# Attention and channel mix on one core: twelve pairs' scores from uncut float32, key-weight work moved to GpSimd, key products from step 7, sums in tiles of their own

## The chip, the cores and the metric

The kernel runs on one NeuronCore of a Trainium2 chip. The metric is the device time of one execution in microseconds (us), the median of three runs: 1001.76 us for the kernel before.

## The reference

```python
def _attn_ref(q, k, v, cap):                       # (8, 12, 448, 64) each
    scale = 1.0 / np.sqrt(q.shape[-1])
    scores = scale * np.matmul(q, k.transpose(0, 1, 3, 2))
    scores = cap * np.tanh(scores / cap)
    scores = scores - np.max(scores, axis=-1, keepdims=True)
    attn = np.exp(scores)
    attn = attn / (np.sum(attn, axis=-1, keepdims=True) + 1e-09)
    return np.matmul(attn, v)
def _moe_ref(x, mu_k, mu_r, w_k, w_v, w_r):        # x: (8, 448, 768)
    x_prev = np.concatenate([np.zeros((B, 1, D)), x[:, :-1, :]], axis=1)
    xk = mu_k * x + (1.0 - mu_k) * x_prev
    xr = mu_r * x + (1.0 - mu_r) * x_prev
    k = np.maximum(xk @ w_k, 0.0)                  # w_k: 768 x 1024
    v = k * k @ w_v                                # w_v: 1024 x 768
    r = 1.0 / (1.0 + np.exp(-(xr @ w_r)))          # w_r: 768 x 768
    return r * v
```

The attention's result, heads side by side, is the x of the second part. The three weight matrices arrive as float64 and are rounded to float32 on the chip.

## The kernel before

**Steps.** Two heads make a pair; 8 batches of 6 pairs give 48 pairs. `run` goes through 54 steps. Step i computes the scores of pair i, the product with the values of pair i-1, and the normalisation and mixing of pair i-2. What a step issues, and in what order, is written out in the strings `EVEN` and `ODD`; every engine works through its own share in that order.

**Scores.** Keys lie on the partitions of the result: three groups `g` of 128 keys (`scores`, L200) and a left group of 64 keys, done for two pairs at once in even steps (`scores_left`, L212). Each half of 64 partitions is one head. The operands are cut in a high and a low part of reduced precision (F32R) by `qk_high` and `qk_low` on GpSimd (for the first pair on VectorE), two steps ahead, and a group is three products: high x high, low x high, high x low. The left group and the product with the values (`values`, L237) use full float32, which the profile shows as two instructions per product. Scores stand in two PSUM tiles that take turns.

**Softmax.** ScalarE does tanh (L218) and exp (L228) of each group over 896 columns; VectorE sums blocks of 32 columns in transposed form (`red`, L252). `gather` (four DMAs on SP's queue at the head of the next step) brings the four partition blocks of the sums together, `recip` adds and inverts them, `rec_store` and `rec_load` spread the result through DRAM, and `norm` (L281) scales the values product. Sums of two pairs share one tile `r1`, and two such tiles take turns.

**Mixing and keys.** `mix_old` (ScalarE, L291) and `mix_new` (VectorE) make xk of the pair; `x_high` and `x_low` cut it on GpSimd (tiles `xkh`, `xkl`). The key products (`kpart`, L331) run over 8 column blocks `fc` of w_k, 6 pairs `dc` and 3 parts: 144 for each batch, 1152 in all. The order inside a batch takes, for the first two blocks, the products of the first five pairs first (15 + 15), then those of the sixth. Four groups of key products, written `K`, stand in each step, and `key_split` says how many products each holds. Two PSUM tiles take turns for the sums over `dc`; ScalarE empties each with a relu.

**Weights.** The weights come in 44 pieces of 128 x 384, 16 of them of w_k. Every step loads one (`weight_load`), `more` loads a second one in some odd steps. ScalarE takes the absolute value at the step's end, VectorE rounds in five operations in the next step (`weight_round`, one for each `f`, the rest in `weight_rest`; L390 is the clamp), GpSimd adds the low word and copies the high part of w_k (`weight_sum`, L405), and VectorE makes its low part one step later (`weight_low`, L418). One tile `wt` holds the clamped value.

**Second phase.** After the steps 28 chunks of 128 rows compute r and v (L474) and the output. `Body(maxima=True)` is a second path for larger caps; it does not run with these inputs.

Of the kernel before, what the change touches and what calls it, by code (L numbers as in the profile page):

```python
# [25 lines left out]
P = 128  # L26
# [11 lines left out]
QM = S + KM  # L38
QA = QM + KL
NSTEP = NPAIR + 6  # L40
HALF = (slice(0, 64), slice(64, 128))
NB = 2 * S // 32

# [8 lines left out]
ODD = """gather load_v weight_load more weight_low S0 S1 V S2 f f f f f weight_rest tanh0 exp0 red0  # L52
# [8 lines left out]
class Body:  # L61
# [61 lines left out]
    def init_sums(self, pool):  # L123


        nc = self.nc
        self.r1, self.sq, self.sr = [], [], []
        for j in range(2):
            self.r1.append(pool.tile([P, 7, NB], F32, name=f"r1_{j}"))
            sq = pool.tile([32, 4, 4, NB], F32, name=f"sq_{j}")  # L130
            g, q = (0, 0) if j else (3, 2)
            nc.gpsimd.memset(sq[:, q + 1, g], 0.0)
            nc.vector.tensor_copy(sq[:, q, g], self.grd[0:32].to_broadcast([32, NB]))
            self.sq.append(sq)
            self.sr.append(pool.tile([32, 32], F32, name=f"sr_{j}"))
            nc.gpsimd.memset(self.sr[j], 1.0)

    def init_attn(self):
        self.raw, self.QK, self.rawv, self.S, self.P32, self.PV, self.R, self.rs = ({} for _ in range(8))
# [30 lines left out]

    def row_maxima(self, i):

        nc, qk, raw = self.nc, self.QK[i], self.raw[i]
        m = self.up.tile([S // 4, 8], F32, name="m", bufs=1)
        for h in range(2):
            t = HALF[h]
            for c in range(4):
                if c % 2 == 0:
                    s = self.ps_s.tile([P, 2, 512], F32, name="s")
                o = s[0:S // 4, c % 2, 0:S]  # L180
                q = slice(c * S // 4, (c + 1) * S // 4)
                for n, (a, b) in enumerate(((0, 0), (1, 0), (0, 1))):
                    nc.tensor.matmul(o[:, 0:KM], qk[b][t, q], qk[a][t, S:QM], start=(n == 0), stop=(n == 2))
                nc.tensor.matmul(o[:, KM:S], raw[t, q], raw[t, QM:QA], start=True, stop=True)
                nc.vector.reduce_max(m[:, 4 * h + c:4 * h + c + 1], o, axis=mybir.AxisListType.X)
        nc.scalar.activation(m, m, AF.Tanh, scale=self.scl_t[0:S // 4])
        nc.vector.tensor_scalar(m, m, self.cap_t[0:S // 4], None, op0=ALU.mult)
        nc.sync.dma_start(self.max_d.rearrange("h (c p) -> p (h c)", c=4), m)
        M = self.M[i] = self.rawp.tile([P, 2, S], F32, name="M")
        for h in range(2):  # L190
            nc.sync.dma_start(M[:, h], self.max_d[h:h + 1, :].to_broadcast([P, S]))

    def scores(self, i, g):
        nc, qk = self.nc, self.QK[i]
        s = self.ps_s.tile([P, 2, 512], F32, name="s")
        k = slice(S + g * P, S + (g + 1) * P)

        for n, (a, b) in enumerate(((0, 0), (1, 0), (0, 1))):
            for h, p in enumerate(HALF):
                nc.tensor.matmul(s[:, h, 0:S], qk[a][p, k], qk[b][p, 0:S], start=(n == 0), stop=(n == 2))  # L200
        if g == 2:
            self.QK.pop(i)
        self.S[i, g] = s

    def scores_left(self, i):


        s = self.ps_s.tile([P, 2, 512], F32, name="s")
        for p in range(2):
            raw = self.raw.pop(i + p)  # L210
# [38 lines left out]


    def red(self, i, g):
        self.nc.vector.tensor_reduce(out=self.r1[i // 2 % 2][:, 3 if g == "L" else i % 2 * 4 + g],  # L252
                                     in_=self.P32[i, g].rearrange("p h (b k) -> p (h b) k", k=32),
                                     axis=mybir.AxisListType.X, op=ALU.add, apply_transpose=True)

    def gather(self, i):
        r1, sq = self.r1[i // 2 % 2], self.sq[i % 2]
        for q in range(4):
            left = int(q // 2 == i % 2)
            g, w = (4 - left, 3 + left) if i % 2 else (0, 3 + left)  # L260
            self.nc.sync.dma_start(sq[:, q, 4 - w:4] if i % 2 else sq[:, q, 0:w], r1[32 * q:32 * q + 32, g:g + w])  # L261

    def recip(self, i):
        nc, t = self.nc, self.sr[i % 2]
        nc.vector.tensor_reduce(out=t[:, 0:NB], in_=self.sq[i % 2].rearrange("l q g x -> l x q g"),  # L265
                                axis=mybir.AxisListType.XY, op=ALU.add)
# [111 lines left out]
    def weight_round(self):  # L378

        nc = self.nc  # L380
        while True:
            if not self.w_abs:
                yield
                continue
            n, w, sq = self.w_abs.pop(0)
            low, top = w[:, :, 0], w[:, :, 1]
            t = self.wp.tile([P, WC], F32, name="wt")
            a = self.wp.tile([P, WC], U32, name="wa", bufs=3)
            u = t.bitcast(U32)
# [12 lines left out]

    def weight_sum(self, e="p"):
        for n, a, sq in self.w_sum:
            {"p": self.nc.gpsimd, "v": self.nc.vector}[e].tensor_add(sq, f(a), sq)  # L405
            if n < NWK:
                fc, d = divmod(n, ND // 3)
                hi, lo = (x[:, 3 * d:3 * d + 3, fc * P:(fc + 1) * P] for x in (self.WKH, self.WKL))
                sq = sq.rearrange("p (c n) -> p c n", c=3)
                self.copy(e, hi, sq)  # L410
                self.w_low.append((lo, sq, hi))
            else:
                self.w_done.append((n, sq))
        self.w_sum = []

    def weight_low(self):
        for lo, sq, hi in self.w_low:
            self.nc.vector.tensor_sub(lo, sq, f(hi))  # L418
        self.w_low = []

    def weight_store(self):
        for n, sq in self.w_done:
# [71 lines left out]
    def step(self, i):  # L494
# [10 lines left out]
        for op in (EVEN if even else ODD).split():  # L505
# [43 lines left out]
    def run(self):  # L549
# [6 lines left out]
        self.w_raw, self.w_abs, self.w_sum, self.w_low, self.w_done = [], [], [], [], []  # L556
        with ExitStack() as outer:
            def pool(name, bufs, stack=outer, **kw):
                return stack.enter_context(tc.tile_pool(name=name, bufs=bufs, **kw))
# [36 lines left out]
            w2p_a = None  # L596
# [1 line left out]
            for i in range(NSTEP):  # L598
                if i == NPAIR + 1:
                    self.weight_store()  # L600
                    assert self.w_next == NW and not (self.w_raw or self.w_abs or self.w_sum or self.w_low)
                    wst.close()
                    est.close()
                    ast.close()
# [90 lines left out]
```

## Time and profile before

| What | Value |
|---|---|
| Median of three runs | 1001.76 us (1000.11 to 1002.43) |
| Profiled execution, its own time | 1000.05 us |
| Span of the profile, first to last instruction | 998.0 us |
| TensorE busy | 944.5 us (95%) |
| VectorE busy | 650.6 us (65%) |
| ScalarE busy | 488.0 us (49%) |
| GpSimd busy | 278.6 us (28%) |

Busy time is the share in which an engine runs at least one instruction. PE is TensorE's matmuls, PEld its weight loads, DVE VectorE, ACT ScalarE, POOL GpSimd, SP the DMA queue of SyncE. Times in the rows below count from the span's start.

### The profile page before, as it was taken

The page shows a single profiled execution, that of the slowest core. Times are in us where ns is not written, and L with a number is a line of the kernel's source. Part 1 is how long each engine was busy: PE and PEld are TensorE (multiplying, and loading weights), DVE is VectorE, ACT ScalarE, POOL GpSimd, SP SyncE. Part 2 cuts the span into 40 slices and gives each one's busy share as a digit, 9 for nine tenths or more (in the row PEclk, how much of TensorE's full clock was granted, in tenths as well). Part 3 has the DMA queues.
Part 4 walks back from the last instruction along what each step waited for, and adds up shares of the span by engine and source line. Part 5 has one row for each costly group of instructions (what it writes and reads, how often), then busy time and mean ns, then how long its engine had stood idle before and what let it go on. Part 6 is the DMA issues. An engine that isn't in the chain of part 4 may idle for free.

```text
span 998.0 us, 14541 instructions
## 1 busy us (share of the span) xinstructions
PE 944.5 (95%) x5328; PEld 754.1 (76%) x5328; DVE 650.6 (65%) x1128; ACT 488.0 (49%) x578; POOL 278.6 (28%) x267
## 2 busy tenths in 40 slices
PE   7667999999999999999999899999999999999997
PEld 3234655666666656656667799999999999999997
DVE  6998987887877777866555486644654554554460
ACT  6776777887878778867675122212211211221220
POOL 4555564445554545444431320000000000000000
PEclk9788999999999999999999999999999999999999
DMA  4545556665665666654433853323332332332220
GB/s 151 164 146 161 166 156 189 191 202 179 195 200 168 196 194 196 200 180 133 145 125 97 269 166 107 106 75 85 106 92 68 106 107 64 96 106 78 82 69 35
DMA packets 124705, 138.52 MB, mean 139 GB/s; under 512 B 19664, under 2 KB 109776, under 8 KB 124624
## 3 DMA queue, kind: packets, MB, share of 16 engines
q1 hardware_dynamic: 115408, 122.82, 42.3%
q10 hardware_dynamic: 9216, 14.68, 4.0%
q8 instruction: 44, 0.72, 0.3%
q14 instruction: 37, 0.30, 0.1%
HBM read 92.64 MB, written 42.40 MB: 135 GB/s over the span
## 4 chain that ended last, share of the span: by engine, by line
PE 71%; DVE 9%; ACT 7%; DMA 6%; issue 2%; SPq 2%; POOL 2%; ACTq 0%; DVEq 0%; POOLq 0%
PE pvv L474 24%; PE pr L474 18%; PE kps L331 15%; PE s L200 6%; PE pv L237 6%; ACT p L228 3%; ACT p L218 3%; DVE r L252 2%; SPq L261 2%; DMA sq<-r 1%; PE pv L246 1%; DMA r<-rec_d 1%; DVE sr L265 1%; PE s L212 1%; DVE x L281 1%
## 5 line engine op out<-in xcount | busy, mean ns | idle before, releaser
L252 DVE TRANSPOSE_TENSOR_REDUCE r<-p 128x28 f32<-128x896 f32 x144 | 158.2, 1105 | 60.6 <-ACT p L228 60.0
L79 ACT CAST xh<-t 128x768 fp32r<-128x768 f32 x27 | 22.6, 838 | 308.4 <-DVE t L457 308.4
L331 PE MATMUL kps<-xkh,wkh 128*128 128x448 f32 x384 | 142.6, 371 | 18.5 <-POOL xkh L75 15.9
L218 ACT ACTIVATE p<-s,scl_t 128x896 f32<-128x896 f32 x144 | 143.4, 996 | 20.6 <-PE s L200 14.1
L228 ACT ACTIVATE p<-p,cap_t 128x896 f32<-128x896 f32 x144 | 149.9, 1041 | 4.0
L331 PE MATMUL kps<-xkl,wkh 128*128 128x448 f32 x384 | 143.9, 375 | 4.9 <-POOL xkl L85 4.9
L489 DVE TENSOR_TENSOR o<-pvv,rsg 128x768 f32<-128x768 f32 (+1 forms) x29 | 27.0, 930 | 184.3 <-PE pvv L474 183.4
L331 PE MATMUL kps<-xkh,wkl 128*128 128x448 f32 x384 | 143.3, 373 | 0.0
L237 PE MATMUL pv<-p,rv 128*64 128x448 f32 x576 | 128.7, 585 | 4.0 <-DVE xk L296 4.0
L474 PE MATMUL pvv<-wvh,kl 128*128 128x384 f32 x448 | 115.8, 336 | 0.0
L474 PE MATMUL pvv<-wvh,kh 128*128 128x384 f32 x448 | 115.7, 336 | 0.0
L474 PE MATMUL pvv<-wvl,kh 128*128 128x384 f32 x448 | 115.6, 336 | 0.0
L331 PEld LDWEIGHTS kps<-xkh,wkh 128*128 128x128 f32 x384 | 72.6, 189 | 29.4 <-POOL xkh L75 20.4
L85 POOL TENSOR_TENSOR qkl<-rqk,qkh 128x832 fp32r<-128x832 f32 x47 | 92.9, 1976 | 3.9
L237 PEld LDWEIGHTS pv<-p,rv 128*64 128x64 f32 x576 | 39.7, 146 | 71.7 <-issue 58.3
L331 PEld LDWEIGHTS kps<-xkl,wkh 128*128 128x128 f32 x384 | 72.5, 189 | 19.7 <-POOL xkl L85 8.3
L405 POOL TENSOR_TENSOR wsq<-wa,wsq 128x384 f32<-128x384 f32 x44 | 44.4, 1009 | 153.4 <-DVE wsq L398 130.3
L474 PE MATMUL pr<-wrl,xh 128*128 128x384 f32 x336 | 85.9, 336 | 0.0
L474 PE MATMUL pr<-wrh,xl 128*128 128x384 f32 x336 | 85.8, 336 | 0.0
L474 PE MATMUL pr<-wrh,xh 128*128 128x384 f32 x336 | 85.8, 336 | 0.0
L200 PE MATMUL s<-qkh 64*128 64x448 f32 x288 | 66.3, 456 | 19.2 <-ACT p L218 12.4
L200 PEld LDWEIGHTS s<-qkh 64*128 64x128 f32 x288 | 28.5, 193 | 71.5 <-issue 25.0
(73 smaller groups left out, 1565.9 us busy)
## 6 DMA issues: line engine op xcount, KB each, us to landing
rqk<-qk SPq DMA_DIRECT2D x47, 448.0 KB
k_d<-ko ACTq DMA_DIRECT2D x64, 224.0 KB
kr<-k_d SPq DMA_DIRECT2D x28, 512.0 KB
x_d<-x SPq DMA_DIRECT2D x48, 224.5 KB
r<-rec_d SPq DMA_DIRECT2D x96, 112.0 KB
out<-o SPq DMA_DIRECT2D x27, 384.0 KB
xc<-x_d SPq DMA_DIRECT2D x24, 387.0 KB
rv<-v SPq DMA_DIRECT2D x48, 192.0 KB
```

Source lines behind the costliest of these rows:

```text
L79: self.nc.scalar.copy(out, x)
L85: {"p": self.nc.gpsimd, "v": self.nc.vector}[e].tensor_sub(*a)
L200: nc.tensor.matmul(s[:, h, 0:S], qk[a][p, k], qk[b][p, 0:S], start=(n == 0), stop=(n == 2))
L218: self.nc.scalar.activation(p32, self.S.pop((i, g))[:, :, 0:S], AF.Tanh, scale=self.scl_t)
L228: self.nc.scalar.activation(p32, p32, AF.Exp, scale=1.0 if self.maxima else self.cap_t)
L237: nc.tensor.matmul(pv[p, 0:S], v[:, g, h, :], ph[:, h, :], start=(g == 0), stop=False)
L252: self.nc.vector.tensor_reduce(out=self.r1[i // 2 % 2][:, 3 if g == "L" else i % 2 * 4 + g], in_=self.P32[i, g].rearrange("p h (b k) -> p ...
L261: self.nc.sync.dma_start(sq[:, q, 4 - w:4] if i % 2 else sq[:, q, 0:w], r1[32 * q:32 * q + 32, g:g + w])
L331: nc.tensor.matmul(self.kps[fc][:, 0:S], w, m[:, dc, :], start=first, stop=last)
L405: {"p": self.nc.gpsimd, "v": self.nc.vector}[e].tensor_add(sq, f(a), sq)
L474: self.nc.tensor.matmul(ps[:, m, 0:HN], a[:, c, :], w[:, c, m * HN:m * HN + HN], start=(c == 0 and part == 0), stop=(c == n - 1 and part = ...
L489: nc.vector.tensor_mul(o[:, q], pv[:, q, 0:HN], rs[:, q])
```

## The change

Five things change. The scores of pairs 0 to 11 read the uncut float32 tiles (`factors`), one product per group and half in place of three, and their `qk_high` and `qk_low` are not issued. For the 16 pieces of w_k the clamp goes to GpSimd, and the low part is made by GpSimd in `weight_sum`, right after the high part; `weight_low` goes. The second piece of a step is loaded in steps 7, 8, 9 and 10 in place of 1, 3, 5, 7 and 9. The key products begin in the first group of step 7 in place of the third group of step 6, and the groups from step 48 on hold 8 in place of 7. The sums of even and odd pairs get a tile each, with the group index innermost; the left sums of the odd pair are copied across by GpSimd, and the four gathers have one form.

```diff
+UNCUT = 12
-EVEN = """gather load_v load_vl weight_load more weight_low S0 S1 V VL L S2 f f f f f weight_rest tanh0 exp0 red0
+EVEN = """gather load_v load_vl weight_load more S0 S1 V VL L S2 f f f f f weight_rest tanh0 exp0 red0
 (ODD: weight_low taken out in the same way)
@@ init_sums
-            self.r1.append(pool.tile([P, 7, NB], F32, name=f"r1_{j}"))
+            self.r1.append(pool.tile([P, NB, 4], F32, name=f"r1_{j}"))
+            self.sq.append(pool.tile([32, 4, NB, 4], F32, name=f"sq_{j}"))
+        self.lz = pool.tile([P, NB], F32, name="lz")
...
@@ scores, row_maxima
+    def factors(self, i):
+        if i < UNCUT:
+            return (self.raw[i],), ((0, 0),)
+        return self.QK[i], ((0, 0), (1, 0), (0, 1))
-        for n, (a, b) in enumerate(((0, 0), (1, 0), (0, 1))):
+        for n, (a, b) in enumerate(terms):
             for h, p in enumerate(HALF):
-                nc.tensor.matmul(s[:, h, 0:S], qk[a][p, k], qk[b][p, 0:S], start=(n == 0), stop=(n == 2))
+                nc.tensor.matmul(s[:, h, 0:S], qk[a][p, k], qk[b][p, 0:S], start=(n == 0), stop=(n == len(terms) - 1))
@@ red, gather
+        r1 = self.r1[0 if g == "L" else i % 2]
+        self.nc.vector.tensor_reduce(out=r1[:, :, 3 if g == "L" else g],
...
+        if g == "L":
+            self.pcopy(self.r1[1][HALF[1], :, 3], r1[HALF[1], :, 3])
+            self.pcopy(r1[HALF[1], :, 3], self.lz[HALF[1]])
         for q in range(4):
+            self.nc.sync.dma_start(self.sq[i % 2][:, q], self.r1[i % 2][32 * q:32 * q + 32])
@@ weight_round, weight_sum
-            nc.vector.tensor_scalar(t, sq, W_TINY, W_HUGE, op0=ALU.max, op1=ALU.min)
+            e = nc.gpsimd if n < NWK else nc.vector
+            e.tensor_scalar(t, sq, W_TINY, W_HUGE, op0=ALU.max, op1=ALU.min)
...
-                self.w_low.append((lo, sq, hi))
+                self.sub(e, lo, sq, f(hi))
-    def weight_low(self):
-        for lo, sq, hi in self.w_low:
-            self.nc.vector.tensor_sub(lo, sq, f(hi))
@@ step
-                if 0 <= j < NPAIR:
+                if 0 <= j < NPAIR and not (op[:2] == "qk" and j < UNCUT):
-                if i in (1, 3, 5, 7, 9):
+                if i in (7, 8, 9, 10):
                     self.weight_load()
@@ key_split
-        for c in range(26, NSTEP * 4):
+        for c in range(28, NSTEP * 4):
             i = c // 4
-            w = min(7 if i % 2 == 0 or i >= NPAIR else 5, total - n)
+            w = min(8 if i >= NPAIR else 5 if i % 2 else 7, total - n)
@@ run
-            self.qk_high(0, "v")
-            self.qk_low(0, "v")
-            self.qk_high(1)
-            self.qk_low(1)
```

## Rows read from the trace of the kernel before

**Rows 1.** Busy time by stretch; columns: stretch, length, each engine, clock, DMA share, GB/s.

```profile
12.07:82.04 69.97, 46.20 (x242) 20.40 (x243) 63.89 (x104) 51.57 (x60) 39.37 (x41) 0.81 0.48 141
82.04:141.21 59.17, 55.62 (x299) 35.58 (x298) 52.26 (x85) 42.16 (x53) 31.49 (x33) 0.93 0.55 168
141.21:530.71 389.50, 378.44 (x2185) 246.96 (x2184) 290.61 (x441) 301.85 (x358) 187.00 (x169) 0.99 0.58 177
178.33:244.27 65.94, 63.97 (x373) 41.78 (x373) 51.84 (x82) 51.85 (x62) 33.39 (x30) 1.00 0.62 188
...
530.71:556.93 26.22, 22.59 (x118) 15.29 (x117) 10.03 (x16) 9.02 (x12) 5.15 (x7) 1.00 0.45 143
556.93:998.00 441.07, 435.50 (x2464) 432.91 (x2464) 228.66 (x470) 76.75 (x91) 9.91 (x9) 0.99 0.35 99
```

**Rows 2.** TensorE's largest wait over the whole span: total us, times, longest.

```profile
PE kps L331 <- POOL xkh L75: 15.9, 9, 5.6
```

**Rows 3.** ScalarE's waits in the first 155 us.

```profile
ACT pv L291 <- DVE x L281: 22.3, 10, 4.6
...
ACT wsq L370 <- DMA w<-wk: 3.6, 5, 1.5
```

**Rows 4.** Timeline of TensorE, steps 15 to 17: start, us, operation.

```profile
178.33 0.47 PE L200 MATMUL s<-qkh 64*128 64x448 f32 x2
...
179.05 0.37 PE L200 MATMUL s<-qkh 64*128 64x448 f32 x2
...
179.76 2.48 PE L237 MATMUL pv<-p,rv 128*64 128x448 f32 x12
182.16 0.47 PE L200 MATMUL s<-qkh 64*128 64x448 f32 x2
...
187.22 0.47 PE L200 MATMUL s<-qkh 64*128 64x448 f32 x2
...
191.84 0.93 PE L212 MATMUL s<-rqk 64*64 64x448 f32 x8
...
199.38 0.47 PE L200 MATMUL s<-qkh 64*128 64x448 f32 x2
```

**Rows 5.** Timeline of VectorE and ScalarE, step 0 and steps 2 to 4.

```profile
4.74 1.03 DVE L85 TENSOR_TENSOR qkl<-rqk,qkh 128x832 fp32r<-128x832 f32 x1
...
6.98 1.01 ACT L218 ACTIVATE p<-s,scl_t 128x896 f32<-128x896 f32 x1
...
34.84 1.04 ACT L228 ACTIVATE p<-p,cap_t 128x896 f32<-128x896 f32 x1
...
43.33 1.03 ACT L228 ACTIVATE p<-p,cap_t 128x896 f32<-128x896 f32 x1
...
55.30 0.64 ACT L291 ACTIVATE pv<-x,om_k 128x448 f32<-128x448 f32 x1 [3.63 <-DVE x L281]
...
57.83 1.04 ACT L228 ACTIVATE p<-p,cap_t 128x896 f32<-128x896 f32 x1
```

**Rows 6.** Groups by line: busy us, mean ns of one, idle before.

```profile
L252 DVE TRANSPOSE_TENSOR_REDUCE r<-p 128x28 f32<-128x896 f32 x144 | 158.2, 1105 | 60.6 <-ACT p L228 60.0
...
L85 POOL TENSOR_TENSOR qkl<-rqk,qkh 128x832 fp32r<-128x832 f32 x47 | 92.9, 1976 | 3.9
...
L405 POOL TENSOR_TENSOR wsq<-wa,wsq 128x384 f32<-128x384 f32 x44 | 44.4, 1009 | 153.4 <-DVE wsq L398 130.3 <-DMA sq<-r 23.1
...
L75 POOL TENSOR_SCALAR wkh<-wsq 128x384 fp32r<-128x384 f32 x16 | 8.2, 512 | 1.4
```

**Rows 7.** The clamp and the low part: duration in ns min/median/max.

```profile
L390 DVE TENSOR_SCALAR wt<-wsq x44: 317/360/1206, 16.0 to 444.5; 128x384 f32<-128x384 f32 x44
...
L418 DVE TENSOR_TENSOR wkl<-wsq,wkh x16: 515/547/1350, 22.9 to 142.7; 128x384 fp32r<-128x384 f32 x16
```

More of the change, by code (lines that the diff above doesn't have):

```diff
@@ L40 @@
 NSTEP = NPAIR + 6
+UNCUT = 12
 HALF = (slice(0, 64), slice(64, 128))
 NB = 2 * S // 32
-EVEN = """gather load_v load_vl weight_load more weight_low S0 S1 V VL L S2 f f f f f weight_rest tanh0 exp0 red0
+EVEN = """gather load_v load_vl weight_load more S0 S1 V VL L S2 f f f f f weight_rest tanh0 exp0 red0
 weight_sum tanh1 exp1 red1 norm recip rec_store K qk_high qk_low tanhL mix_old mix_new x_high x_low relu k_store
 K expL redL relu k_store K K tanh2 exp2 red2 relu k_store weight_abs load_qk rec_load x_store weight_store"""
-ODD = """gather load_v weight_load more weight_low S0 S1 V S2 f f f f f weight_rest tanh0 exp0 red0
+ODD = """gather load_v weight_load more S0 S1 V S2 f f f f f weight_rest tanh0 exp0 red0
 weight_sum tanh1 exp1 red1 norm recip rec_store K qk_high qk_low tanh2 mix_old mix_new x_high x_low relu k_store
@@ L128, in init_sums @@
         for j in range(2):
-            self.r1.append(pool.tile([P, 7, NB], F32, name=f"r1_{j}"))
[L130 to L134, printed above, removed]
+            self.r1.append(pool.tile([P, NB, 4], F32, name=f"r1_{j}"))
+            self.sq.append(pool.tile([32, 4, NB, 4], F32, name=f"sq_{j}"))
             self.sr.append(pool.tile([32, 32], F32, name=f"sr_{j}"))
             nc.gpsimd.memset(self.sr[j], 1.0)
+        self.lz = pool.tile([P, NB], F32, name="lz")
+        nc.gpsimd.memset(self.lz, 0.0)
+        for q in (0, 2):
+            p = slice(32 * q, 32 * q + 32)
+            nc.vector.tensor_copy(self.lz[p], self.grd[p].to_broadcast([32, NB]))
+        self.pcopy(self.r1[1][HALF[0], :, 3], self.lz[HALF[0]])
     def init_attn(self):
@@ L171, in row_maxima @@
     def row_maxima(self, i):
-        nc, qk, raw = self.nc, self.QK[i], self.raw[i]
+        nc, raw = self.nc, self.raw[i]
+        qk, terms = self.factors(i)
         m = self.up.tile([S // 4, 8], F32, name="m", bufs=1)
@@ L181, in row_maxima @@
                 q = slice(c * S // 4, (c + 1) * S // 4)
-                for n, (a, b) in enumerate(((0, 0), (1, 0), (0, 1))):
-                    nc.tensor.matmul(o[:, 0:KM], qk[b][t, q], qk[a][t, S:QM], start=(n == 0), stop=(n == 2))
+                for n, (a, b) in enumerate(terms):
+                    nc.tensor.matmul(o[:, 0:KM], qk[b][t, q], qk[a][t, S:QM], start=(n == 0), stop=(n == len(terms) - 1))
                 nc.tensor.matmul(o[:, KM:S], raw[t, q], raw[t, QM:QA], start=True, stop=True)
@@ L191, in row_maxima @@
             nc.sync.dma_start(M[:, h], self.max_d[h:h + 1, :].to_broadcast([P, S]))
+    def factors(self, i):
+        if i < UNCUT:
+            return (self.raw[i],), ((0, 0),)
+        return self.QK[i], ((0, 0), (1, 0), (0, 1))
     def scores(self, i, g):
-        nc, qk = self.nc, self.QK[i]
+        nc = self.nc
+        qk, terms = self.factors(i)
         s = self.ps_s.tile([P, 2, 512], F32, name="s")
         k = slice(S + g * P, S + (g + 1) * P)
-        for n, (a, b) in enumerate(((0, 0), (1, 0), (0, 1))):
+        for n, (a, b) in enumerate(terms):
             for h, p in enumerate(HALF):
-                nc.tensor.matmul(s[:, h, 0:S], qk[a][p, k], qk[b][p, 0:S], start=(n == 0), stop=(n == 2))
-        if g == 2:
-            self.QK.pop(i)
+                nc.tensor.matmul(s[:, h, 0:S], qk[a][p, k], qk[b][p, 0:S], start=(n == 0), stop=(n == len(terms) - 1))
         self.S[i, g] = s
@@ L209, in scores_left @@
         for p in range(2):
-            raw = self.raw.pop(i + p)
+            raw = self.raw[i + p]
             for h, t in enumerate(HALF):
@@ L251, in red @@
     def red(self, i, g):
-        self.nc.vector.tensor_reduce(out=self.r1[i // 2 % 2][:, 3 if g == "L" else i % 2 * 4 + g],
+        r1 = self.r1[0 if g == "L" else i % 2]
+        self.nc.vector.tensor_reduce(out=r1[:, :, 3 if g == "L" else g],
                                      in_=self.P32[i, g].rearrange("p h (b k) -> p (h b) k", k=32),
                                      axis=mybir.AxisListType.X, op=ALU.add, apply_transpose=True)
+        if g == "L":
+            self.pcopy(self.r1[1][HALF[1], :, 3], r1[HALF[1], :, 3])
+            self.pcopy(r1[HALF[1], :, 3], self.lz[HALF[1]])
     def gather(self, i):
-        r1, sq = self.r1[i // 2 % 2], self.sq[i % 2]
         for q in range(4):
-            left = int(q // 2 == i % 2)
-            g, w = (4 - left, 3 + left) if i % 2 else (0, 3 + left)
-            self.nc.sync.dma_start(sq[:, q, 4 - w:4] if i % 2 else sq[:, q, 0:w], r1[32 * q:32 * q + 32, g:g + w])
+            self.nc.sync.dma_start(self.sq[i % 2][:, q], self.r1[i % 2][32 * q:32 * q + 32])
     def recip(self, i):
         nc, t = self.nc, self.sr[i % 2]
-        nc.vector.tensor_reduce(out=t[:, 0:NB], in_=self.sq[i % 2].rearrange("l q g x -> l x q g"),
+        nc.vector.tensor_reduce(out=t[:, 0:NB], in_=self.sq[i % 2].rearrange("l q x g -> l x q g"),
                                 axis=mybir.AxisListType.XY, op=ALU.add)
@@ L414, in weight_sum @@
         self.w_sum = []
-    def weight_low(self):
-        for lo, sq, hi in self.w_low:
-            self.nc.vector.tensor_sub(lo, sq, f(hi))
-        self.w_low = []
     def weight_store(self):
@@ L555, in run @@
         self.wl, self.w_next, self.w_used, self.w_goal = 0, 0, 0, 0
-        self.w_raw, self.w_abs, self.w_sum, self.w_low, self.w_done = [], [], [], [], []
+        self.w_raw, self.w_abs, self.w_sum, self.w_done = [], [], [], []
         with ExitStack() as outer:
@@ L600, in run @@
                     self.weight_store()
-                    assert self.w_next == NW and not (self.w_raw or self.w_abs or self.w_sum or self.w_low)
+                    assert self.w_next == NW and not (self.w_raw or self.w_abs or self.w_sum)
                     wst.close()
```

## The prediction

> **What bounds the kernel now.** Four things were read, in this order. First the table by stretch, cut where a step's first score product starts on TensorE, and at 556.93 us, where the key products go on after the last pair's tile [rows 1]. From 556.93 us to the end TensorE is busy 435.5 of 441.07 us: nothing in that stretch is touched, and it is a constant. Before 82.04 us it is busy 46.2 of 69.97 us at a granted clock of 0.81, while VectorE is busy 63.89: another engine sets the pace there. From 141.21 to 530.71 us it is busy 378.44 of 389.5 us.
>
> Second, TensorE's largest wait [rows 2]: the key products wait nine times for the high part of a mixed tile, 15.9 us together, 5.6 at most. Third, what ScalarE waits for in the first 155 us: 22.3 us for `norm` on VectorE (x, L281), ten times [rows 3].
>
> Fourth, two stretches of the timeline. In the clean pair of steps 15 and 16 the scores start at 178.33, 187.22 and 199.38 us [rows 4]: an odd step lasts 8.89 us, an even one 12.16 us, all of it TensorE work. In steps 3 and 4 the last exponentials start at 34.84, 43.33 and 57.83 us [rows 5]: the odd step takes 8.49 us on ScalarE, the even one 14.50 us, and in that even step ScalarE stands 3.63 us before `mix_old`. So the kernel has three regimes: steps 1 to 6 set by VectorE and ScalarE in turn, steps 7 to 11 mixed, steps 12 to 47 set by TensorE plus a wait that comes back every six steps.
>
> **The wait that comes back.** From 141.21 to 530.71 us run steps 12 to 46, 18 even and 17 odd. Clean they would take 18 x 12.16 + 17 x 8.89 = 370.0 us; they take 389.5 [rows 1, 4]. The 19.5 us lost lie at the changes of batch: batch b's first key products stand in the second half of step 6b+6. Product 12 of a batch reads the tile of pair 6b+4 and falls into the last group of step 6b+6; product 30 reads that of pair 6b+5 and falls into the last group of step 6b+7. Each of these tiles is made in that same step, by a chain over ScalarE, VectorE, a DMA round trip and GpSimd, so TensorE stands. Part of the loss comes after the wait: in the six steps from 244.27 us, 67.06 us long where 63.15 would be clean, TensorE stands only 1.8 us and the granted clock is 0.97 [rows 1].
>
> The change starts the key products at step 7. Groups hold 5 in odd steps and 7 in even ones, so steps 7 to 12 do 20 + 28 + 20 + 28 + 20 + 28 = 144, exactly one batch. Product 12 now falls into the third group of step 6b+7, product 30 into the second of step 6b+8: each a step after its tile is made. I take the wait as gone. What is new: product 36 opens a third sum and needs the PSUM tile of the first, whose last product is number 32; the three products between cover 0.6 us (step 15's third score group starts at 182.16 us, takes 0.72, and 20 key products fill the time to 187.22: 0.21 each [rows 4]), and the relu has to fit in there. I put 0.3 us on each of seven batches, 2.1 us; the bounds are nothing and 1 us each. Term: 19.5 - 2.1 = **17.4 us gained** (12 to 19.5).
>
> The 14 products moved behind step 47 cost 14 x 0.21 = 2.9 us of TensorE. There, from 530.71 to 556.93 us, it is busy 22.59 of 26.22 us and waits for the last pair's tile [rows 1], whose chain hangs on the start of step 47 and not on TensorE's queue. The 3.6 us of idle time hide the 2.9. Cost nothing; without that cover, 2.9 us.
>
> **Steps 0 to 6.** Removed per pair, for the first twelve: the cut on GpSimd, of which the low part alone takes 1.98 us [rows 6]. Only at the very start is it on the path: VectorE makes the first pair's low part from 4.74 to 5.77 us and the first tanh starts at 6.98 [rows 5]. Without it the start is earlier by 1.1 us (0.6 to 1.6).
>
> Moved from VectorE, per piece: the clamp, 0.36 us in the middle and 1.21 at most, and the low part, 0.55 in the middle and 1.35 at most [rows 7]. Pieces rounded in steps 1 to 6: nine before, six after, never two in a step. After, an odd step stays at 8.49 us: VectorE no longer leads there, and `norm` waits for the reduction behind the second exponential. An even step has the same ScalarE work plus a tanh and an exponential over the left tile, 1.01 + 1.04 us by the rows of their kind [rows 5]: 10.5 us, in place of 14.50, since what made ScalarE wait, the second piece's rounding, lies before `norm` on VectorE. Three such pairs of steps: 3 x (22.99 - 19.0) = 12.0 us. With the start: **13.1 us gained**.
>
> The bounds. Up: nothing but ScalarE's order, 1 us less per step, 19 us gained. Down: each step may wait for its weight piece to land (3.6 us in five waits so far [rows 3]; the piece is asked for after four gathers, and a shorter step leaves it less time), and the chain norm, recip, store, load, norm, once around per step, has to fit: 1 us more per step, 7 us gained.
>
> The uncut scores are the unknown operation: two halves, each 64 rows x 128 columns in full float32. The nearest row is the value product, float32 too and split in two instructions: 12 in 2.48 us for three key groups [rows 4], 0.8 us per group, against 0.72 us for a cut group (178.33 to 179.05). That row pairs two column halves; the left scores, 8 in 0.93 us [rows 4], show that row halves run together as well. I take 0.8 to 0.9 us. The lower bound is half of it, if eight quadrant products in 0.93 us are the measure; the upper is 1.6 us, if the halves go one after the other. At 0.9 us in steps 1 to 6 TensorE needs under 7 us of every even step, and has the cover.
>
> The small work is free: two copies of 64 x 28 values on GpSimd wait for the left reduction and are done while VectorE reduces the last tile (1.1 us [rows 6]); the gather at the head of SP's queue waits for that reduction anyhow. Bound: the nearest GpSimd copy, 0.51 us for 384 columns, twice in every even step, 1 us, if the gather ends last. A tile of sums returns after two steps instead of four, and its gather is issued a step before the next writer. The gathers stay four per step. The strided result of the reduction has no row; it writes 28 of its 896 values, so I take it as equal (0.1 us per step would be hidden behind TensorE from step 12 on).
>
> **Steps 7 to 11.** They last 59.17 us now [rows 1]. TensorE's floor after the change, with 0.2 us more per score group: 3 x 9.5 + 2 x 12.8 = 54.1 us. VectorE now rounds seven pieces there, at four rounding operations plus clamp and low part; after the change nine (steps 8 to 11 two each), without these two. Each second piece, though, waits for its clamp on GpSimd, which can start only when the first has left the shared tile (0.51 us and the hand-over), and then meets GpSimd's add, 1.01 us [rows 6]. So VectorE's load stays about as it is, and I take **0** (from 5 gained to 5 lost).
>
> Here one rule bears on the case. The clamp's 1.21 us stand against 0.36 us in the middle [rows 7]: it is held up by about one GpSimd operation of 0.9 to 1.0 us. The Trainium skill, SBUF — State Buffer, section "Who interferes with whom", says that GpSimd and VectorE share one port pair, and that a VectorE operation in a two-port mode, or with two SBUF inputs, blocks wholly while a GpSimd operation holds it. The trace agrees for the clamp. By that rule the moved work can come back as blocked time; it is rival 2.
>
> **The sum.** 17.4 + 13.1 + 0 = 30.5 us. The profiled execution took 1000.05 us, so 969.6; the median of the runs shown lies 1.7 us above that execution: **971 us**.
>
> **Rivals.** 1. The batch wait only changes its cause (the relu before the third sum, ScalarE's lag, a late load). For it: the early pace is new, and in steps 12 to 46 both VectorE (290.6 us) and ScalarE (301.9) are busy three quarters. Against: the clean pair of steps shows them keeping up. Then only the early part is gained: 1001.8 - 13.1 = 989 us.
> 2. GpSimd blocks VectorE: the eight pieces of steps 8 to 11 bring their clamp and low part back, 8 x (0.51 + 1.01) = 12.2 us: 983 us. For it the 1.21 us; against it, at least 1.98 us of GpSimd work per pair are gone in steps 0 to 9.
> 3. Early steps as long as before, by the DMA chain or by TensorE at its low clock: 984 us. For it the 0.81 clock; against it, ScalarE's 22.3 us of waits have one named cause, which shrinks.
> 4. The other side: the halves of an uncut score go one after the other and the clock stays at its low level, 3.2 us per group. Then TensorE sets the early pace: six groups 19.2, values 2 x 2 x 2.48, left products 2 x 2 x 0.93, so 33 us per two steps instead of 23, 30 us lost over three pairs, and 5 us in steps 7 to 11 (a floor of 64 us at 1.6 per group); with 17.4 gained: 1019 us. It decides from 1.7 us per group for the early steps, from about 2.7 for the whole. Against it stands the left product's rate.
> 5. Nothing moves: both gains are hidden by something that no view shows: 1002 us.
>
> **Chances.** Forecast 0.58 (its own range 960 to 981), rival 1 0.12, rival 2 0.09, rival 3 0.12, rival 4 0.05, rival 5 0.04. The range reaches to rival 1: 958 to 989. Faster than 0.2% (about what a measurement of this kernel can tell from no change): 0.91; within it 0.04; slower 0.05.
>
> **What the profile after should show.** Scores of steps 0 to 11 as one float32 form, 12 instructions per pair, a group 0.8 to 0.9 us apart. Step 7's scores near 69 us, step 12's near 128, step 47's near 500. From step 12 on, 8.9 and 12.2 us in turn without a seventh step out of line, and waits of key products for the mixed tiles only at the first batch or the last pair. ScalarE's wait for `norm` before step 12 halved. The last stretch from the last pair's tile to the end still 441 us. I am wrong if the uncut group exceeds 1.6 us, if steps 8 to 11 last over 55 us, or if a six-step stretch stays above 65 us.

## The result and the profile after

The changed kernel takes **992.50 us** (median of five runs, 989.87 to 993.63). The kernel before, run between them on the same chip, took 1001.76 (1000.11 to 1003.95). The ratio is 0.9904, with an interval of 0.9885 to 0.9922. So the change gains 9.3 us where 30.5 were forecast, and the time lies 3.5 us above the upper end of the range.

The profiled execution took 993.05 us, its span is 991.2. The table by stretch, cut where TensorE's first score product of steps 1, 7, 13 and 47 starts and where TensorE goes on with the last pair's mixed tile ([rows 1] cut at step 12 in place of 13). Columns: stretch, its length, busy us (and instructions) of TensorE, weight load, VectorE, ScalarE and GpSimd, granted clock, DMA share, GB/s.

```profile
10.85:65.67 54.82, 41.31 (x192) 12.84 (x192) 40.41 (x67) 45.98 (x52) 29.83 (x35) 0.91 0.46 142
65.67:159.30 93.63, 75.18 (x342) 42.36 (x343) 65.23 (x100) 56.39 (x69) 64.44 (x69) 0.89 0.49 147
159.30:519.51 360.21, 360.04 (x2110) 237.56 (x2109) 270.01 (x430) 293.15 (x347) 190.50 (x199) 1.00 0.62 187
519.51:546.71 27.20, 24.90 (x131) 18.07 (x130) 9.41 (x16) 9.21 (x12) 5.15 (x7) 1.00 0.46 143
546.71:991.20 444.49, 436.86 (x2464) 433.30 (x2464) 228.58 (x470) 76.72 (x91) 9.19 (x9) 0.99 0.35 98
```

The second and third of these stretches in the kernel before; the others stand in [rows 1]:

```profile
82.04:153.37 71.33, 67.78 (x375) 43.59 (x374) 62.92 (x100) 52.00 (x64) 39.02 (x40) 0.95 0.56 168
153.37:530.71 377.34, 366.27 (x2111) 238.95 (x2110) 279.96 (x425) 292.01 (x346) 179.46 (x162) 0.99 0.58 177
```

Beside the five stretches of the kernel before (70.0, 71.3, 377.3, 26.2 and 441.1 us), three things stand out. Steps 1 to 6 are 15.2 us shorter. Steps 13 to 46 are 17.1 us shorter, and TensorE is busy in 360.04 of their 360.21 us. Between the two, steps 7 to 12 are 22.3 us longer: that is where the forecast went. No engine is full there. GpSimd is busy in 69% of the stretch, against 54 and 53% in its neighbours. TensorE stands 18.5 us in place of 3.6, and its granted clock falls to 0.89, from 0.95.

The largest waits in steps 7 to 12, all engines (us in total, times, longest); [rows 2, 3] show the largest waits of TensorE and ScalarE before, over longer stretches:

```profile
ACT pv L301 <- DVE x L291: 26.8, 6, 6.7
DVE wa L403 <- POOL wt L401: 19.8, 10, 3.7
POOL wsq L416 <- DVE wsq L409: 10.2, 7, 2.1
...
POOL wt L401 <- DVE wsq L409: 8.8, 4, 2.2
PE kps L341 <- ACT ko L348: 7.5, 2, 4.1
...
PE pv L246 <- DVE xk L306: 6.0, 2, 4.2
...
PE s L211 <- ACT p L227: 4.9, 2, 4.3
```

VectorE waits ten times for the clamp on GpSimd (L401). GpSimd waits four times for the shared tile before a second clamp. ScalarE stands 26.8 us before `mix_old` for `norm`, once in each of the six steps, and TensorE waits 7.5 us for relus that are queued behind that `mix_old`, 6.0 for `mix_new` and 4.9 for a tanh: nearly all of the 18.5 us. VectorE's longest wait, 3.69 us in step 12, has a third part beside the clamp's duration and the tile: the clamp stands in GpSimd's own queue, behind the mixed tile's low part, and starts at 148.92 us, though its input is ready at 147.05.

Step 10 shows how. Timeline of the changed kernel, VectorE, ScalarE and GpSimd: start, duration, engine, line, tiles, and the idle time before with what ended it.

```profile
113.02 1.11 DVE L262 TRANSPOSE_TENSOR_REDUCE r<-p 128x28 f32<-128x896 f32 x1
...
114.98 1.49 POOL L401 TENSOR_SCALAR wt<-wsq 128x384 f32<-128x384 f32 x1
...
116.50 0.36 DVE L403 TENSOR_SCALAR wa<-wt 128x384 uint32<-128x384 uint32 x1 [2.38 <-POOL wt L401]
...
116.90 0.56 DVE L405 SCALAR_TENSOR_TENSOR wa<-w,wa 128x384 uint32<-128x384 uint32 x1
117.49 0.36 DVE L407 TENSOR_SCALAR wt<-wa 128x384 uint32<-128x384 uint32 x1
...
117.96 0.56 DVE L409 SCALAR_TENSOR_TENSOR wsq<-w,wt 128x384 f32<-128x384 uint32 x1
118.67 1.49 POOL L401 TENSOR_SCALAR wt<-wsq 128x384 f32<-128x384 f32 x1 [2.20 <-DVE wsq L409]
...
120.13 1.02 POOL L416 TENSOR_TENSOR wsq<-wa,wsq 128x384 f32<-128x384 f32 x1
120.19 1.17 DVE L403 TENSOR_SCALAR wa<-wt 128x384 uint32<-128x384 uint32 x1 [1.68 <-POOL wt L401]
...
121.40 0.75 DVE L405 SCALAR_TENSOR_TENSOR wa<-w,wa 128x384 uint32<-128x384 uint32 x1
121.83 1.19 POOL L86 TENSOR_TENSOR wkl<-wsq,wkh 128x384 fp32r<-128x384 f32 x1
122.19 1.06 DVE L407 TENSOR_SCALAR wt<-wa 128x384 uint32<-128x384 uint32 x1
123.35 0.56 DVE L409 SCALAR_TENSOR_TENSOR wsq<-w,wt 128x384 f32<-128x384 uint32 x1
123.82 2.10 DVE L262 TRANSPOSE_TENSOR_REDUCE r<-p 128x28 f32<-128x896 f32 x2
...
125.84 0.59 DVE L291 TENSOR_TENSOR x<-pv,r 128x448 f32<-128x448 f32 x1
...
126.47 0.64 ACT L301 ACTIVATE pv<-x,om_k 128x448 f32<-128x448 f32 x1 [6.74 <-DVE x L291]
```

The clamp takes 1.49 us on GpSimd, three times the 0.51 us that the prediction took from the copy row [rows 6]. VectorE stands idle meanwhile (2.38 us): the next operation in the order that the kernel gives it reads the clamp's result. The second clamp starts only when the first piece's last rounding operation has read the shared tile (118.67), and VectorE waits again. Then the second piece's rounding meets GpSimd's add and low part: 1.17, 0.75 and 1.06 us, where the first piece took 0.36, 0.56 and 0.36. `norm` ends late, and ScalarE stands 6.74 us.

The standing also makes what follows slower. In step 12 TensorE waits 4.16 us, until VectorE is through with the second piece of step 11, and the value products behind this wait take 4.75 us where [rows 4] show 2.48. The granted clock of that stretch is 0.50, the lower of the two levels (1.2 GHz):

```profile
145.68 4.75 PE L246 MATMUL pv<-p,rv 128*64 128x448 f32 x12 [4.16 <-DVE xk L306]
```

What went as forecast: TensorE's timeline of steps 15 to 17 (to be held against [rows 4]). The scores start 8.89 and 12.19 us apart.

```profile
180.65 0.47 PE L211 MATMUL s<-qkh 64*128 64x448 f32 x2
...
189.54 0.47 PE L211 MATMUL s<-qkh 64*128 64x448 f32 x2
...
201.73 0.47 PE L211 MATMUL s<-qkh 64*128 64x448 f32 x2
```

And one uncut score group in step 8, TensorE's timeline: two products in four instructions from 88.06 us, the next key product at 89.01, so 0.95 us.

```profile
88.06 1.02 PE L211 MATMUL s<-rqk 64*128 64x448 f32 x4
89.01 0.47 PE L341 MATMUL kps<-xkl,wkh 128*128 128x448 f32 x1
```

### The profile page after: what moved, and what is told of

It is laid out like the page before. It is cut to its first block, busy times and chain, and to the rows that moved or that the text cites. A ratio compares the mean times of both kernels' runs of the same rounds, so it can differ in the third digit from the quotient of the medians.

```text
span 991.2 us, 14491 instructions
## 1 busy us (share of the span) xinstructions
PE 944.1 (95%) x5256; PEld 746.0 (75%) x5256; DVE 617.0 (62%) x1094; ACT 488.0 (49%) x578; POOL 299.8 (30%) x325
## 4 chain that ended last, share of the span: by engine, by line
PE 80%; DVE 7%; DMA 4%; ACT 3%; SPq 2%; POOL 2%; issue 2%; ACTq 0%; DVEq 0%; POOLq 0%
PE pvv L480 23%; PE kps L341 19%; PE pr L480 17%; PE pv L246 9%; PE s L211 8%; PE pv L255 2%; DVE r L262 2%; PE s L221 1%; DMA sq<-r 1%; POOL wt L401 1%; SPq L271 1%; DMA wst<-w_d 1%; ACT p L227 1%; ACT p L237 1%; DMA w<-wk 1%
## 5 line engine op out<-in xcount | busy, mean ns | idle before, releaser
L341 PE MATMUL kps<-xkh,wkh 128*128 128x448 f32 x384 | 145.3, 378 | 9.5 <-ACT ko L348 7.5
L246 PE MATMUL pv<-p,rv 128*64 128x448 f32 x576 | 126.3, 576 | 7.9 <-DVE xk L306 7.8
L480 PEld LDWEIGHTS pvv<-wvh,kh 128*128 128x128 f32 x448 | 81.3, 188 | 0.0
L480 PEld LDWEIGHTS pvv<-wvh,kl 128*128 128x128 f32 x448 | 81.3, 188 | 0.0
L480 PEld LDWEIGHTS pvv<-wvl,kh 128*128 128x128 f32 x448 | 81.3, 188 | 0.0
```

The source lines that it names most:

```text
L246: nc.tensor.matmul(pv[p, 0:S], v[:, g, h, :], ph[:, h, :], start=(g == 0), stop=False)
L341: nc.tensor.matmul(self.kps[fc][:, 0:S], w, m[:, dc, :], start=first, stop=last)
L480: self.nc.tensor.matmul(ps[:, m, 0:HN], a[:, c, :], w[:, c, m * HN:m * HN + HN], start=(c == 0 and part == 0), stop=(c == n - 1 and part = ...
```

## The experiments

Theory A: VectorE stands behind GpSimd's clamp, by its duration and by the hand-over through one tile. Theory B: two pieces in each of steps 8 to 11 are too much for VectorE, whoever clamps. All versions side by side; the stretches are those of the first table, in us of the profiled execution, and the ratio is against the kernel before, run beside each group of versions (its medians lie between 1000.97 and 1002.11 us).

| version | median us | steps 1–6 | 7–12 | 13–46 | 47 to last tile | after it | ratio (interval) |
|---|---|---|---|---|---|---|---|
| before | 1001.76 | 70.0 | 71.3 | 377.3 | 26.2 | 441.1 | |
| changed | 992.50 | 54.8 | 93.6 | 360.2 | 27.2 | 444.5 | 0.9904 (0.9885–0.9922) |
| e1 clamp on VectorE | 976.92 | 53.4 | 80.3 | 360.2 | 26.8 | 444.5 | 0.9742 (0.9708–0.9776) |
| e3 two clamp tiles | 983.79 | 54.7 | 84.9 | 361.4 | 26.2 | 443.1 | 0.9818 (0.9783–0.9853) |
| e9 one compare | 985.65 | 53.3 | 87.8 | 361.4 | 25.6 | 443.9 | 0.9838 (0.9803–0.9872) |
| e4 old steps for pieces | 997.24 | 66.7 | 86.9 | 360.2 | 26.4 | 442.8 | 0.9951 (0.9936–0.9966) |
| e8 e1 and e4 | 980.83 | 61.4 | 75.8 | 360.2 | 26.7 | 443.7 | 0.9787 (0.9770–0.9805) |
| e10 e8, low part back | 979.45 | 61.0 | 75.3 | 360.3 | 27.6 | 444.2 | 0.9778 (0.9758–0.9798) |
| e5 before, keys from step 7 | 985.30 | 63.0 | 74.7 | 360.8 | 27.0 | 444.2 | 0.9829 (0.9813–0.9846) |
| e6 changed, keys as before | 1006.74 | 60.5 | 90.8 | 371.5 | 25.5 | 443.3 | 1.0047 (1.0030–1.0063) |
| e7 changed, all scores cut | 1003.11 | 60.5 | 97.6 | 361.2 | 24.8 | 444.7 | 1.0008 (0.9997–1.0019) |
| e12 e1, pieces 2, 4, 6, 8 | 977.05 | 61.6 | 70.9 | 360.2 | 26.5 | 443.0 | 0.9761 (0.9744–0.9779) |
| e13 e1, pieces 4, 6, 8, 10 | 975.81 | 58.2 | 72.8 | 360.2 | 26.1 | 446.3 | 0.9741 (0.9719–0.9763) |
| e14 e13, sums as before | 978.76 | 59.2 | 74.9 | 359.6 | 27.2 | 445.8 | 0.9775 (0.9754–0.9795) |

**e1: only the clamp goes back to VectorE.**

```
-            e = nc.gpsimd if n < NWK else nc.vector
+            e = nc.vector
```

> The changed kernel with the clamp of the 16 key-weight pieces back on VectorE; all else as changed. Theory A (VectorE stands behind GpSimd's clamp, 1.49 us each, twice in a step in steps 8 to 11): steps 7 to 12, from TensorE's first score product of step 7 to that of step 13, last about 80 us in place of 93.6, and the median is 977 to 982 us. Theory B (two pieces rounded in each of four steps are too much for VectorE, whoever clamps): at most 4 us less, 988 us or more.

Measured 976.92 us, 15.6 less than the changed kernel; 13.3 of them in steps 7 to 12, which last 80.3 us where theory A had about 80. The same step 10, VectorE's timeline of e1:

```profile
105.19 1.11 DVE L262 TRANSPOSE_TENSOR_REDUCE r<-p 128x28 f32<-128x896 f32 x1
106.64 0.66 DVE L401 TENSOR_SCALAR wt<-wsq 128x384 f32<-128x384 f32 x1 [0.34 <-ACT wsq L380]
107.34 0.36 DVE L403 TENSOR_SCALAR wa<-wt 128x384 uint32<-128x384 uint32 x1
...
109.38 1.18 DVE L401 TENSOR_SCALAR wt<-wsq 128x384 f32<-128x384 f32 x1
...
111.20 1.27 DVE L405 SCALAR_TENSOR_TENSOR wa<-w,wa 128x384 uint32<-128x384 uint32 x1
...
115.40 0.59 DVE L291 TENSOR_TENSOR x<-pv,r 128x448 f32<-128x448 f32 x1
```

From the end of the reduction to `norm` it is now 9.10 us (106.30 to 115.40) in place of 11.71 (114.13 to 125.84). The wait of ScalarE in steps 7 to 12, from e1's table of waits, falls by 10.4 us:

```profile
ACT pv L301 <- DVE x L291: 16.4, 6, 4.1
```

VectorE's clamp is no cheap one here either (1.18 us beside GpSimd's add), and still it wins. TensorE has the very same products in e1; the stretch reads:

```profile
64.66:144.97 80.31, 69.83 (x342) 39.64 (x342) 68.76 (x109) 56.35 (x69) 49.04 (x58) 0.96 0.57 173
```

Against 75.18 us busy of 93.63 at a clock of 0.89, about 8 of the 13.3 us are TensorE standing less, and about 5 are the same products done faster. Theory A has the larger part; B's part is what is left, below.

**e3: the clamp's tile twice, so that a second clamp need not wait.**

```
-            t = self.wp.tile([P, WC], F32, name="wt")
+            t = self.wp.tile([P, WC], F32, name="wt", bufs=2)
```

> The changed kernel with two tiles for the clamped value in place of one, so that the second clamp of a step need not wait until VectorE has done with the first. Theory A with the hand-over as its larger part: about 3 us less in each of steps 8 to 11, 979 to 983 us. Theory A with the clamp's own time and the shared port as its larger part: VectorE's first wait stays and its operations meet GpSimd's clamp instead, 986 to 991 us. Theory B: no change, 992 us.

Measured 983.79 us, 8.7 less than the changed kernel. The two clamps of step 8 now run back to back, and VectorE starts its second piece at once (timeline of e3):

```profile
82.71 2.94 POOL L401 TENSOR_SCALAR wt<-wsq 128x384 f32<-128x384 f32 x2
...
84.23 0.65 DVE L403 TENSOR_SCALAR wa<-wt 128x384 uint32<-128x384 uint32 x1 [2.12 <-POOL wt L401]
...
86.44 0.35 DVE L403 TENSOR_SCALAR wa<-wt 128x384 uint32<-128x384 uint32 x1
86.83 1.24 DVE L405 SCALAR_TENSOR_TENSOR wa<-w,wa 128x384 uint32<-128x384 uint32 x1
```

The wait for the first clamp (2.12 us) stays, so e3 reaches a little over half of e1's gain. The time falls between the two ranges given for theory A: the hand-over has about half, not clearly the larger part.

**e9: the same chain with a cheaper clamp.** GpSimd's pieces are clamped from below alone; the upper bound is left out.

```
-            e.tensor_scalar(t, sq, W_TINY, W_HUGE, op0=ALU.max, op1=ALU.min)
+            e.tensor_scalar(t, sq, W_TINY, None, op0=ALU.max)    # on GpSimd
```

> The changed kernel with GpSimd's clamp of the key weights cut to its lower bound alone: one maximum, no minimum (this leaves out the upper bound of the clamp). It measures what GpSimd's two compare operations cost. If the price lies in the kind of operation, not in the width, one of them takes 0.75 to 1.0 us in place of 1.49 and the median falls to 984 to 988 us; if each GpSimd operation of this width has the price of the copy, 0.5 us and 980 us. Theory B: 991 to 993 us.

Measured 985.65 us, 6.9 less than the changed kernel, for 16 clamps that are 0.32 us shorter each, 5.2 us together. The view of the tile (minimum, median and maximum in ns, first and last start), first of the changed kernel, then of e9:

```profile
L401 POOL TENSOR_SCALAR wt<-wsq x16: 1488/1489/1492, 14.5 to 148.9; 128x384 f32<-128x384 f32 x16
```

```profile
L401 POOL TENSOR_SCALAR wt<-wsq x16: 1162/1164/1170, 14.5 to 144.1; 128x384 f32<-128x384 f32 x16
```

One compare cost more than the 0.75 to 1.0 us expected, and the median is in the range. So the duration of the clamp is paid in full, as far as the intervals tell, and GpSimd's price for it depends on the kind of operation: 0.51 us for the copy's multiply and add, 1.16 for one compare, 1.49 for two, all on 128 x 384 values. In these two runs the spread within one kind is at most 0.01 us.

**e4 and e8: the pieces in their old steps,** e4 with the clamp on GpSimd, e8 with it on VectorE.

```
-                if i in (7, 8, 9, 10):
+                if i in (1, 3, 5, 7, 9):
```

> The changed kernel with the second pieces loaded in steps 1, 3, 5, 7 and 9 again, in place of 7 to 10. Theory A: the same 16 clamps on GpSimd cost about the same wherever they are, early steps take 9 us more and steps 7 to 12 10 to 14 us less, 987 to 992 us. Theory B: the bunch in steps 8 to 11 is gone, 980 to 985 us.

> The clamp back on VectorE and the second pieces in steps 1, 3, 5, 7 and 9 again; low part, scores and key products as changed. With the clamp away from GpSimd the place of the pieces is worth little by theory A: 975 to 982 us. By theory B spreading them is worth as much as the clamp: under 970 us. If the lighter early steps are the gain of the shifted pieces, they are lost here: 984 to 988 us.

Measured 997.24 and 980.83 us. e4 is slower than either theory had it: steps 7 to 12 get 6.7 us shorter, where 10 to 14 were expected, and steps 1 to 6 11.9 longer. GpSimd's clamp costs wherever the piece stands: 16.4 us with the old steps (e4 against e8), 15.6 with the new ones (the changed kernel against e1). e8 lies in theory A's range, far above theory B's. In e8 against e1, with the clamp on VectorE, the same shift costs 8.0 us early and gives 4.5 back later: 61.4 against 53.4, then 75.8 against 80.3. So theory B holds for 4.5 us of steps 7 to 12; over the whole kernel the bunch is no loss (976.92 against 980.83, with intervals that overlap a little).

**e10: e8 with the low part on VectorE, a step later, as before the change.**

```
+    def weight_low(self):
+        for lo, sq, hi in self.w_low:
+            self.nc.vector.tensor_sub(lo, sq, f(hi))
+        self.w_low = []
...
-                self.sub(e, lo, sq, f(hi))
+                self.w_low.append((lo, sq, hi))
```

> As the run with the clamp on VectorE and the second pieces in steps 1 to 9, but with the low part of the key weights back on VectorE too, one step later as before. It prices the low part's move by itself, against 980.8 us. If taking 16 low parts of 0.55 to 1.35 us from VectorE is what the move is worth: 987 to 992 us. If GpSimd's 1 us each costs as much in blocked VectorE time: 979 to 983 us.

Measured 979.45 us beside e8's 980.83; the intervals overlap. With the clamp on VectorE, the move of the low part is worth nothing that these runs can tell.

**e5 and e6: the start of the key products alone,** e5 put into the kernel before, e6 taken out of the changed one.

```
-        for c in range(26, NSTEP * 4):
+        for c in range(28, NSTEP * 4):
...
-            w = min(7 if i % 2 == 0 or i >= NPAIR else 5, total - n)
+            w = min(8 if i >= NPAIR else 5 if i % 2 else 7, total - n)
```

> The kernel before with one part of the change alone: the key products start in step 7, with the changed group sizes. If the wait at the change of batch hangs on where the products stand (the term of 17.4 us), steps 12 to 47 run clean at 8.9 and 12.2 us and the median is 982 to 987 us. If that wait only changes its cause, the time stays at 998 us or more.

> The changed kernel with the key products from the third group of step 6 again, with the old group sizes. By the same term the waits for the mixed tiles come back at each change of batch, 14 to 18 us more from step 13 to step 47, and the median is 1004 to 1010 us. If the wait had only changed its cause: 990 to 995 us.

Measured 985.30 and 1006.74 us. This edit alone gives 16.8 us on the kernel before (1002.11 beside it), more than the whole change; without it the changed kernel is slower than before. In e6 steps 13 to 46 grow by 11.3 us, less than the 14 to 18 expected. From step 13 to step 46 TensorE's waits hold none for a mixed tile in the changed kernel and in e5; in e6 they are back:

```profile
PE kps L341 <- POOL xkh L76: 5.2, 6, 0.9
PE kps L341 <- POOL xkl L86: 3.3, 6, 0.6
```

**e7: every score from cut operands again.**

```
-UNCUT = 12
+UNCUT = 0
```

The two cuts of the first pairs ahead of the loop come back with it.

> The changed kernel with all scores from cut operands again, the first pair cut on VectorE at the start as before. If the uncut scores give what I took them for (the start, and 2.87 us of GpSimd time per pair in steps 0 to 9 that nothing waits for), the median is 993 to 996 us. If GpSimd's time in these steps is what bounds them, each step before the tenth grows by 1 to 3 us: 1002 to 1015 us. If the uncut products cost TensorE more than they save, 985 to 990 us.

Measured 1003.11 us, 10.6 more than the changed kernel: 5.7 in steps 1 to 6 and 3.9 in steps 7 to 12. With the clamp in GpSimd's queue, GpSimd's cut of the pairs is no longer free. With the clamp on VectorE the uncut scores were not taken out by themselves, but e10 differs from e5 in nothing but the uncut scores and the sums' layout, and the two together give about 5 us there (0.9829 to 0.9778).

**e12 and e13: e1 with the pieces spread over every second step.**

```
-                if i in (7, 8, 9, 10):
+                if i in (2, 4, 6, 8):       # e12; e13 has (4, 6, 8, 10)
```

> Clamp on VectorE, second pieces loaded in steps 2, 4, 6 and 8, so that two pieces are rounded in the odd steps 3, 5, 7 and 9, which hold no left scores. If the doubled rounding costs most where an even step already has the longer chain to norm: 968 to 974 us. If only the number of doubled steps counts: 976 to 981 us.

> Clamp on VectorE, second pieces loaded in steps 4, 6, 8 and 10, rounded in pairs in steps 5, 7, 9 and 11. As the run before, with half of the pairs under key products that TensorE has to do anyway: 966 to 973 us by the first view, 975 to 979 us by the second.

Measured 977.05 and 975.81 us, both in the ranges of the second view: from e1 neither can be told apart. What spreading saves late it costs early: steps 1 to 12 together take 133.7 us in e1, 132.5 in e12 and 131.0 in e13. e13 is the fastest median of all versions, 0.9741 of the kernel before, and beats both kernels, as e1 does.

**e14: e13 with the layout of the key sums as before the change** (`init_sums`, `red`, `gather` and `recip`).

```
-        r1 = self.r1[0 if g == "L" else i % 2]
-        self.nc.vector.tensor_reduce(out=r1[:, :, 3 if g == "L" else g],
+        self.nc.vector.tensor_reduce(out=self.r1[i // 2 % 2][:, 3 if g == "L" else i % 2 * 4 + g],
...
```

> As the run with pairs in steps 5, 7, 9 and 11, but with the sums in two shared tiles as before the change (no copies on GpSimd, gathers and the adding reduction in the old layout). If the new layout costs nothing, as I predicted: within 2 us of that run. If the shorter adding reduction (0.59 us in place of 0.95 to 1.0) is worth something in the steps that VectorE sets: 2 to 6 us more. If the copies and the longer gathers cost: 2 to 4 us less.

Measured 978.76 us against e13's 975.81; the intervals (0.9754 to 0.9795 and 0.9719 to 0.9763) overlap a little. A gain of some 3 us from the sums' own tiles is likely, and not settled.

**The parts in a row.** Five of these versions lead from the kernel before to the changed one: the key products' start takes the ratio from 1 to 0.9829 (e5), uncut scores and the sums' layout to 0.9778 (e10), the low part on GpSimd to 0.9787 (e8), the pieces in steps 7 to 10 to 0.9742 (e1), and the clamp on GpSimd back to 0.9904. The intervals set the first, the second and the last of these moves apart; the third and the fourth are not clear of noise.

## Why the prediction failed

By its own steps, with the terms of its sum:

| step | forecast | measured | verdict |
|---|---|---|---|
| the batch wait, steps 12 to 46 | 17.4 gained | 17.1 gained in steps 13 to 46, 16.5 there by e5 alone; step 12 is counted below | right |
| start and steps 1 to 6 | 13.1 gained | 1.2 + 15.2 = 16.4 gained | 3.3 too small, and partly luck |
| steps 7 to 11 | 0, from 5 gained to 5 lost | 15.2 lost, and 7.1 in step 12 behind them: 22.3 | **the step that failed** |
| 14 products behind step 47 | 0 | 1.0 lost | right as far as can be told: 24.8 to 27.6 us in all versions |
| after the last tile | constant | 3.4 lost | wrong, small |

The measured terms add up to 6.8 us, the difference of the two profiled executions' spans, 998.0 and 991.2; the medians differ by 9.3, because the profiled execution of before lay 1.7 us under its median and that of after 0.55 above.

**The step that failed** is the price of the second piece: "0.51 us and the hand-over", set against VectorE's relief from clamp and low part. The 0.51 us is the row of a copy on GpSimd [rows 6], which the prediction took without saying why a clamp should cost the same. The clamp has the same tile, shape and engine but another operation, and takes 1.49 us. The first piece of every step pays too: VectorE's wait before it is 2.38 us in step 10, where e1 waits 0.34 us and clamps in 0.66. The hand-over was named but never worked out in microseconds; e3 removes the wait for the shared tile, and 8.7 us go. The bound of 5 us lost came from no row. The loss reaches past step 11, since TensorE's step 12 waits for VectorE's work of step 11. Taken apart in the order of the versions, in the 22.3 us stand 13.3 for the clamp's place (changed against e1), 4.5 for two pieces in a step (e1 against e8) and 4.5 that e8 has over the kernel before, most of it the later start of the key products, which by itself takes 3.4 (e5).

Rival 2 was right in kind: GpSimd holds VectorE in steps 8 to 11. It priced the wrong part. It let clamp and low part come back as blocked time, 12.2 us; e10 shows no difference for the low part's place (with the clamp on VectorE), and e1, e3 and e9 show that most of the loss is VectorE waiting for the clamp's result. Operations that meet on the two engines are the lesser part: beside GpSimd's add and low part three rounding operations last 1.17, 0.75 and 1.06 us in place of 0.36, 0.56 and 0.36, 1.7 us per second piece. e1, which keeps such overlaps (1.18 and 1.27 us), is the faster all the same; no run takes them away, so their own price is not shown. The Trainium skill, SBUF — State Buffer, section "Who interferes with whom", says that a VectorE operation in a two-port mode, or with two SBUF inputs, waits while GpSimd holds the port pair that the two share. These rows agree with it.

The measured 992.5 us lie next to rival 1's 989, but not by its mechanism, for the batch wait went as forecast. Its relay appears as a consequence: TensorE waits 7.5 us for two relus in steps 7 to 12, since ScalarE's queue stands before `mix_old`; in e1 it is 3.5, in the kernel before 2.5. From step 13 on one even step of each batch lasts 12.48 us in place of 12.19: the 0.3 us per batch that the prediction put on the relu before the third sum. TensorE's weight loads wait six times for a relu there, 2.4 us together.

**What was right, and what was luck.** The batch wait was right in mechanism and size: no wait for a mixed tile is left from step 13 to 46, and of the 17.1 us some 11 are waits that are gone and 6 the same products done faster, at a granted clock of 1.00 in place of 0.99. The row of the six steps from 244.27 us, which the prediction reads and [rows 1] leave out, shows both parts at one change of batch:

```profile
244.27:311.33 67.06, 65.24 (x375) 42.54 (x374) 52.86 (x82) 52.22 (x63) 33.38 (x30) 0.97 0.63 195
```

The key product's 0.21 us should read 0.22 (4.34 us for 20), which moves no term by more than 0.2 us. In the early steps ScalarE's wait came from the second piece's rounding, as claimed, but putting the pieces back (e8 against e1) costs 8.0 of the 12.0 us forecast. Another 7.0 come from the key products' start (70.0 to 63.0 us in e5, nearly all of it in step 6, which falls from 18.07 to 11.53), and the prediction counted nothing for it there. That the stage came out near the forecast is luck. The start itself, 1.2 us against 1.1, and the uncut group, 0.95 us against 0.8 to 0.9, came out close. Step 7's first score stands at 65.67 us against "near 69", step 12's at 140.03 against 128. Of the prediction's signs of being wrong one came: steps 8 to 11 last over 55 us, namely 57.8. ScalarE's wait for `norm` did not halve: it was 22.3 us in the first 155 us [rows 3], and is 26.8 in steps 7 to 12 alone.

**Mis-sized without harm:** the cuts' removal was priced at 1.1 us, at the start. In the changed kernel it is worth 10.6 (e7), with the clamp in GpSimd's queue behind such work, as in step 12.

**Left open:** the stretch behind the last tile is 441.1 us in the kernel before and 442.8 to 446.3 in all others, e5 among them, which changes only the key products' start. Two short waits at its head are all that TensorE's waits of the changed kernel name there, 1.9 us together; it is also busy 1.4 us longer (436.86 against 435.50 us), with as many products:

```profile
PE pr L480 <- ACT xh L80: 1.2, 1, 1.2
PE pr L480 <- DVE xl L471: 0.7, 2, 0.5
```

What makes these tiles late, and the products slower, was not tried.

## What to carry to other kernels

An operation moved to GpSimd should be priced by a row of the same kind of operation on GpSimd, not by one of the same shape; where there is none, the bound must reach to the dearest row there is, times every instruction moved. Where its result goes straight back to the engine that it was taken from, the wait for that result belongs in the sum: here it cost far more than the relief, and one shared tile made more than half of the cost (8.7 of 15.6 us). A change of several parts deserves a run of each part alone: here one part gave 16.8 us, more than the whole, and another took 15.6 back.

## What the hardware showed unexpectedly

GpSimd's time for one 128 x 384 float32 operation with constants runs from 0.51 us (multiply and add) over 1.16 (one compare) to 1.49 (two compares), the same within 0.01 us in all 16 pieces of the changed kernel and of e9; VectorE does the two compares in 0.36 us when undisturbed [rows 7]. Layout alone speeds up VectorE's adding reduction over the gathered sums: with the four terms side by side in memory it takes 594 ns, where before 48 instructions took 48.2 us, 1003 ns each; e14, which only brings the old layout back, has 1011 ns. The group of the changed kernel (busy us, mean ns, idle before):

```profile
L275 DVE TENSOR_REDUCE sr<-sq 32x28 f32<-32x448 f32 x48 | 28.5, 594 | 9.5 <-DMA sq<-r 9.3
```
